# Scores with keys on partitions, transposes by DMA: a change to a fused memory-attention, mixer and MLP kernel

## The chip, the cores and the metric

The kernel runs on one core of one Trainium2 chip. The metric is the time of one execution on the device, in microseconds (us), as the median of several runs; lower is better. One run of each kernel was taken with the hardware profiler; stage lengths and waits come from that run, and its span is a microsecond or two below the time of that run.

Engine names in the profile: PE is TensorE (matmuls), PEld its weight loads, DVE VectorE, ACT ScalarE, POOL GpSimd, SP SyncE, which does nothing here but issue DMA transfers. A name with a q (SPq, ACTq) is the engine's instruction queue issuing a DMA.

## The reference, cut to what matters

```python
# x: 2048 tokens x 1024; 32 heads of 128; 64 segments of 32 tokens, 8 memory slots
h = layernorm(x) * (1 + ca) + sa
mem = mem0
for s in range(64):                                  # recurrent over segments
    hs = concat([mem, h[segment s]])                 # 40 rows
    q, k, v = hs @ Wq, hs @ Wk, hs @ Wv              # per head
    p = softmax(where(mask, q @ k.T * scale, -1e9))
    o = (p @ v) @ Wo
    mem, out[segment s] = o[:8], o[8:]
x1 = x + ga * out
u = layernorm(x1) * (1 + cb) + sb
# the "mixer": w1, gelu, a shift of channel groups by 1 or 2 tokens, w2
x1b = u + shift(gelu(layernorm(u) @ w1)) @ w2
y  = x1b + gelu(layernorm(x1b) @ w3) @ w4            # the last MLP, 1024 -> 3584 -> 1024
result = x1 + gb * y
# sa, ca, ga, sb, cb, gb: six rows of 1024, from silu(c) @ w_mod
```

The recurrence is removed in both kernels: all memories are guessed from segment means, all segments are computed at once with one memory column a segment (its eight rows are taken to be equal), and a check at the end decides whether an exact pass must follow. With these inputs none follows.

## The kernel before: the parts that matter here

Tokens and memory columns of three segments form a tile of 99 columns; there are 22 tiles a head. Two heads ("a pair") share one load of projection weights. TensorE gets attention work of one pair woven with the projections of the next.

```python
# V token-major: hh is the stationary operand, 256 columns (a pair of heads) move
nc.tensor.matmul(a3[:rows, j, :], lhsT=hhT[:, kt, tokens i], rhs=w["wv"][:, kt, :], ...)
evac(vs[...], a3[...])                                # PSUM -> staging tile
nc.sync.dma_start(V[p0:p0 + e - n, T, :], vs[n - i * P:e - i * P, j, :])   # L502: to tiles of 99 rows
# --- cut ---
# scores: queries on partitions, softmax along the free axis, 5 tiles a group
nc.tensor.matmul(ps_s[:TS, b, :], lhsT=QT[tile], rhs=KTt[tile])
nc.vector.tensor_tensor(smk, ps_s, mask, ALU.add)                          # L558
nc.vector.tensor_reduce(nmx, smk, AX.X, ALU.max, negate=True)              # L560
for b in range(nb):
    nc.scalar.activation(E[:, b], smk[:, b], ACT.Exp, bias=nmx[:, b:b+1], accum_out=ssum[:, b:b+1])  # L564
nc.vector.reciprocal(rin, ssum)
nc.vector.tensor_tensor(Pm, E, rin, ALU.mult)
nc.tensor.transpose(ps_t[tile], Pm[tile], ident)                           # L578
nc.vector.tensor_copy(PT, ps_t)                                            # L580
nc.tensor.matmul(ps_o[tile], lhsT=V[tile], rhs=PT[tile])                   # feature-major output
# --- cut: outputs copied to stgx / OTm4 and written to DRAM (OTx_d) ---
# Wo stage: OTc reads the head outputs back, 32 heads accumulate, then LayerNorms give z
for kt in range(KT): nc.tensor.transpose(pt[:, kt, :], z[:, kt * P:(kt + 1) * P], ident)   # L758
nc.vector.tensor_copy(zT[tile t], pt)
# modulation rows: silu(c) repeated over 128 columns is the stationary operand
for kt in range(KT): nc.tensor.matmul(pb, lhsT=sc_rep[:, kt, :], rhs=wm[:, kt, :], ...)
```

## Time and profile before

The kernel before takes 1675.88 us (median of 3 runs, 1674.5 to 1677.36). This is the profile's page for it: the span, the busy time and share of each engine with its number of instructions, then the span in 40 slices of about 42 us, each digit the busy share in tenths (for PEclk, the granted TensorE clock).

```profile
span 1674.0 us, 30157 instructions
...
PE 1607.6 (96%) x11426; PEld 924.5 (55%) x11601; DVE 692.5 (41%) x1688; ACT 681.8 (41%) x2202; POOL 222.4 (13%) x324
...
PE   6898999999999999999998989999999999999998
...
PEclk9998999999999999999998999999999999999999
```

TensorE is busy nearly always, and the others under half of the time. The digits that are not 9 show where time can be lost without TensorE working: at the start, in the fourth slice (about 126 to 167 us, where attention begins), and in slices 22 and 24 (between about 880 and 1005 us, where attention ends and the output projection begins). The stretch table gives busy microseconds and instruction counts of each engine in stretches of 100 us, then the granted clock and the DMA share.

```profile
core 0: us, PE busy (x) PEld busy (x) DVE busy (x) ACT busy (x) POOL busy (x), PEclk, DMA share, GB/s
...
100.00:200.00 100.00, 91.01 (x919) 70.27 (x923) 35.21 (x93) 51.59 (x196) 18.56 (x41) 0.95 0.42 123
...
300.00:400.00 100.00, 98.76 (x867) 66.39 (x878) 56.06 (x147) 60.67 (x231) 1.67 (x10) 1.00 0.32 86
...
900.00:1000.00 100.00, 89.28 (x477) 42.78 (x486) 34.04 (x103) 25.89 (x86) 24.11 (x35) 0.94 0.77 265
```

In the middle of attention TensorE is the limit (the missing matmul records, told of below, make its 98.76 a little too low), so what leaves TensorE there leaves the time. The groups of instructions say what TensorE and ScalarE do for the softmax and for V (columns: line, engine, operation, tiles, shapes, count; busy us and mean ns of one; idle time before them and what ended it).

```profile
L487 PE MATMUL acc<-wv,hhT 128*128 128x256 bf16 (+1 forms) x2176 | 265.6, 275 | 0.7 <-DVE hhT L405 0.7
L564 ACT ACTIVATE E<-smk,nmx 99x99 f32<-99x99 f32 x704 | 256.4, 367 | 124.9 <-DVE nmx L560 122.6 <-DVE OTm_2212 L601 0.8 <-DVE rin L570 0.6
...
L578 PE MATMUL ps_t<-ident,Pm 99*99 99x99 bf16 x704 | 61.4, 214 | 4.7 <-POOL Pm L572 3.4 <-DVE Pm L572 1.0
```

A mean duration is not what a matmul costs when they are pipelined. The 704 transposes show 214 ns each, but their starts are about 47 ns apart. In this trace the start spacing is 216 ns at 512 columns, 109 at 256, 56 at 128, 47 at 99: columns divided by 2.4 per ns, plus about 2.5 ns. The Trainium skill says the same (TensorE: Matmul & The Clock Gate, Part 1: "N ÷ 2.4 GHz + ≈2.5 ns once warm", with 215.7 ns at 512 columns); the trace agrees.

### The profile page before, as it was taken

The page shows a single profiled execution, that of the slowest core. Times are in us where ns is not written, and L with a number is a line of the kernel's source. Part 1 is how long each engine was busy: PE and PEld are TensorE (multiplying, and loading weights), DVE is VectorE, ACT ScalarE, POOL GpSimd, SP SyncE. Part 2 cuts the span into 40 slices and gives each one's busy share as a digit, 9 for nine tenths or more (in the row PEclk, how much of TensorE's full clock was granted, in tenths as well). Part 3 has the DMA queues.
Part 4 walks back from the last instruction along what each step waited for, and adds up shares of the span by engine and source line. Part 5 has one row for each costly group of instructions (what it writes and reads, how often), then busy time and mean ns, then how long its engine had stood idle before and what let it go on. Part 6 is the DMA issues. An engine that isn't in the chain of part 4 may idle for free. (4 is left out here: it accounts for less than half of the span.)

```text
span 1674.0 us, 30157 instructions
## 1 busy us (share of the span) xinstructions
PE 1607.6 (96%) x11426; PEld 924.5 (55%) x11601; DVE 692.5 (41%) x1688; ACT 681.8 (41%) x2202; POOL 222.4 (13%) x324
## 2 busy tenths in 40 slices
PE   6898999999999999999998989999999999999998
PEld 3477666666666666666665434444444444444443
DVE  5614446555465554645555153453285020111102
ACT  2515657566566665655657020222423203021120
POOL 6301200000000000000002132032012304040300
PEclk9998999999999999999998999999999999999999
DMA  9682334232242422335314897776177767474741
GB/s 316 220 278 71 95 85 109 70 95 80 62 108 70 111 64 74 95 107 157 113 35 144 288 326 267 266 252 220 44 256 247 257 187 246 150 263 136 235 132 50
DMA packets 251868, 267.20 MB, mean 160 GB/s; under 512 B 11354, under 2 KB 221370, under 8 KB 249666
## 3 DMA queue, kind: packets, MB, share of 16 engines
q1 hardware_dynamic: 241136, 236.57, 45.8%
q10 hardware_dynamic: 9938, 26.51, 4.0%
q8 instruction: 93, 1.52, 0.4%
q0 software_dynamic: 640, 2.10, 0.4%
q14 instruction: 61, 0.50, 0.1%
HBM read 205.54 MB, written 42.23 MB: 148 GB/s over the span
## 5 line engine op out<-in xcount | busy, mean ns | idle before, releaser
L564 ACT ACTIVATE E<-smk,nmx 99x99 f32<-99x99 f32 x704 | 256.4, 367 | 124.9 <-DVE nmx L560 122.6
L487 PE MATMUL acc<-wv,hhT 128*128 128x256 bf16 (+1 forms) x2176 | 265.6, 275 | 0.7 <-DVE hhT L405 0.7
L248 PE MATMUL acc<-hhT,wq 128*128 128x512 bf16 (+3 forms) x1264 | 252.4, 341 | 8.3 <-DVE hhT L344 2.1
L248 PE MATMUL acc<-hhT,wk 128*128 128x512 bf16 (+3 forms) x1262 | 252.8, 340 | 2.5
L679 PE MATMUL acc<-wstream,OTc 128*128 128x512 bf16 x999 | 228.6, 384 | 12.9 <-DMA wstream<-in_A_Wo_dram 7.5
L487 PEld LDWEIGHTS <-hhT 128*128 128x128 bf16 (+1 forms) x2176 | 211.1, 100 | 31.8 <-DVE hhT L405 1.2
L883 PE MATMUL acc<-z2T,wstream 128*128 128x512 bf16 x878 | 193.1, 379 | 0.9
L907 PE MATMUL acc<-wstream,h2T 128*128 128x512 bf16 x878 | 193.1, 379 | 0.9
L884 ACT ACTIVATE h2T<-acc 128x512 bf16<-128x512 f32 x112 | 66.9, 597 | 270.9 <-PE acc L883 266.2
L248 PEld LDWEIGHTS <-wq 128*128 128x128 bf16 x1312 | 113.1, 98 | 112.0 <-issue 6.2
L248 PEld LDWEIGHTS <-wk 128*128 128x128 bf16 x1312 | 113.0, 98 | 110.0 <-DMA wk<-in_A_Wk_dram 1.8
L679 PEld LDWEIGHTS <-OTc 128*128 128x128 bf16 x1024 | 100.1, 99 | 130.7 <-issue 15.5
L907 PEld LDWEIGHTS <-h2T 128*128 128x128 bf16 x896 | 87.7, 98 | 105.7
L883 PEld LDWEIGHTS <-wstream 128*128 128x128 bf16 x896 | 87.6, 98 | 105.5
L564 ACT ACTIVATION_READ_ACCUMULATOR E<-smk,nmx 99x1 f32 x704 | 132.1, 188 | 0.0
L570 DVE RECIPROCAL rin<-ssum 99x5 f32<-99x5 f32 (+1 forms) x160 | 29.5, 184 | 197.8 <-ACT E L564 197.5
L560 DVE TENSOR_REDUCE nmx<-smk 99x5 f32<-99x495 f32 (+1 forms) x160 | 96.6, 604 | 2.2
L580 DVE COPY PT<-ps_t 99x495 bf16<-99x495 bf16 (+1 forms) x160 | 61.7, 386 | 83.5 <-PE ps_t L578 81.5
L598 ACT CAST stgx<-ps_o 128x480 bf16<-128x480 f32 (+2 forms) x160 | 80.1, 501 | 35.9 <-PE ps_o L593 34.4
L98 ACT ACTIVATE QT<-acc 128x512 bf16<-128x512 f32 (+2 forms) x126 | 65.1, 522 | 67.9 <-PE acc L248 64.5
L96 ACT CAST vstg<-acc 128x512 bf16<-128x512 f32 (+1 forms) x111 | 61.1, 551 | 74.1 <-PE acc L487 57.2
L96 ACT CAST KTt<-acc 128x512 bf16<-128x512 f32 (+3 forms) x121 | 60.6, 513 | 58.4 <-PE acc L248 51.1
(337 smaller groups left out, 1546.7 us busy)
## 6 DMA issues: line engine op xcount, KB each, us to landing
wstream<-in_A_Wo_dram SPq DMA_DIRECT2D x36, 1024.0 KB
wstream<-in_B_w_dram SPq DMA_DIRECT2D x28, 1024.0 KB
wstream<-in_B_w_dram SPq DMA_DIRECT2D x32, 896.0 KB
OTx_d<-stgx SPq DMA_DIRECT2D x32, 512.0 KB
OTc<-OTx_d SPq DMA_DIRECT2D x16, 1024.0 KB
wstream<-in_w_mod_dram SPq DMA_DIRECT2D x9, 1024.0 KB
wq<-in_A_Wq_dram SPq DMA_DIRECT2D x16, 512.0 KB
wk<-in_A_Wk_dram SPq DMA_DIRECT2D x16, 512.0 KB
```

The costliest lines, as they stand in the source:

```text
L96: nc.scalar.copy(dst, src)
L98: nc.scalar.mul(dst, src, scale)
L248: nc.tensor.matmul(acc[:, o:o + n], lhsT=W[:, kt, hl * P:(hl + 1) * P], rhs=rhs_fn(kt), start=(kt == 0), stop=(kt == KT - 1))
L487: nc.tensor.matmul(a3[:rows, j, :], lhsT=hhT[:, kt, O0 + i * P:O0 + i * P + rows], rhs=w["wv"][:, kt, :], start=(kt == 0), stop=(kt == KT ...
L560: nc.vector.tensor_reduce(nmx[:TS, :nb], smk[:TS, :nb, :], AX.X, ALU.max, negate=True)
L564: nc.scalar.activation(E[:TS, b, :], smk[:TS, b, :], ACT.Exp, bias=nmx[:TS, b:b + 1], scale=1.0, accum_out=ssum[:TS, b:b + 1])
L580: nc.vector.tensor_copy(g["PT"][:TS, :nb, 0:TS], ps_t[:TS, :nb, 0:TS])
L598: nc.scalar.copy(stgx[:].rearrange("p (s j) -> p s j", j=SEG)[:, s0:s0 + nsg, :], blk[:, b0:3 * nb, MS:L])
L679: nc.tensor.matmul(accs[tt][:], lhsT=ot[:, hl, tt * P:(tt + 1) * P], rhs=woc[:, hl, :], start=(h == 0), stop=(h == H - 1))
L883: nc.tensor.matmul(acc[:], lhsT=w3c[:, kt, fl * P:(fl + 1) * P], rhs=z2T[:, kt, b * 512:(b + 1) * 512], start=(kt == 0), stop=(kt == KT - 1))
L884: nc.scalar.activation(h2T[:, ft, :], acc[:], ACT.Gelu_apprx_tanh)
L907: nc.tensor.matmul(accs[tt][:], lhsT=h2T[:, ft, tt * P:(tt + 1) * P], rhs=w4c[:, fl, :], start=(ft == 0), stop=(ft == FT - 1))
```

## The change

The intent is to take work from TensorE in attention and to thin out the softmax on ScalarE and VectorE.

- Scores are computed with keys on partitions, so the masked exponentials are already in the form that the output product needs as its stationary operand: no transpose of the probabilities. No maximum is subtracted, the mask is a product with 0, 1 or 8, and the row sum comes out as a 129th column of the output product (a column of ones beside V). One wide exponential serves five tiles.
- V is projected feature-major, like Q and K (weights stationary, 480 tokens move), and turned by a DMA transpose, one a head. The head output is token-major now and is turned by two DMA transposes. The 608 DMA copies from staging tiles into V are gone.
- Tokens are permuted so that a tile is 96 tokens in a row, followed by its 3 memory columns.
- The transposes of z, in both mixer products, become DMA transposes on ScalarE's queue.
- The modulation rows are summed on VectorE, split into two bf16 halves, and spread over partitions by two matmuls instead of eight.

```diff
@@ V and projections (cut) @@
-    nc.tensor.matmul(a3[:rows, j, :], lhsT=hhT[:, kt, tokens i], rhs=w["wv"][:, kt, :], ...)
-    nc.sync.dma_start(V[p0:p0 + e - n, T, :], vs[n - i * P:e - i * P, j, :])
+    nc.tensor.matmul(acc[:, 0:CH], lhsT=W[:, kt, hl * P:(hl + 1) * P], rhs=hh[:, kt, i * CH:(i + 1) * CH], ...)
+    nc.sync.dma_start_transpose(Vs[h % 3][:, :, 0:DH], VTs[h % 2][:].rearrange("p t c -> p (t c)"))
@@ scores and softmax (cut) @@
-    nc.tensor.matmul(ps_s[:TS, b, :], lhsT=QT[...], rhs=KTt[...])
-    ... add mask, max, 5 exponentials with row sums, reciprocal, multiply, transpose, copy ...
+    nc.tensor.matmul(ps[:rows, o:o + w], lhsT=KTt[:, ...], rhs=QT[:, ...])
+    nc.scalar.activation(E[:rows, 0:o], ps[:rows, 0:o], ACT.Exp)
+    nc.vector.tensor_tensor(Em[:rows, c0:c0 + o], E[:rows, 0:o], mk[:rows, 0:o], ALU.mult)
@@ outputs (cut) @@
-    nc.tensor.matmul(ps_o[...], lhsT=V[:TS, T, ...], rhs=PT[:TS, b, 0:TS])
+    nc.tensor.matmul(ps[:rows, i, :], lhsT=Em[:k, ...], rhs=V[:k, t, 0:DH + 1])
+    nc.vector.reciprocal(rin, ps[:rows, 0:n, DH])
+    nc.vector.tensor_tensor(O[:rows, ...], ps[:rows, 0:n, 0:DH], rin[...], ALU.mult)      # Os: 2 buffers
+    # flip(h), after the last outputs of the head:
+    nc.sync.dma_start_transpose(OT, O[0:96, :, :].rearrange("p t c -> p (t c)"))
+    nc.sync.dma_start_transpose(MT, O[96:112, :, :].rearrange("p t c -> p (t c)"))
@@ z (cut) @@
-    for kt in range(KT): nc.tensor.transpose(pt[:, kt, :], z[:, kt * P:(kt + 1) * P], ident[:])
-    nc.vector.tensor_copy(dstT[:, :, t * P:(t + 1) * P], pt[:])
+    nc.scalar.dma_start_transpose(z2T[:, :, t * P:(t + 1) * P], zs[t][:])
@@ modulation rows (cut) @@
-    for kt in range(KT): nc.tensor.matmul(pb[:], lhsT=sc_rep[:, kt, :], rhs=wm[:, kt, :], ...)
+    nc.vector.scalar_tensor_tensor(a, wm[:, kt, :], sc32[:, kt:kt + 1], a, ALU.mult, ALU.add)   # x8
+    # hi = bf16(a); lo = a - hi
+    nc.tensor.matmul(pb[:], lhsT=ones_b[:], rhs=hi, start=True, stop=False)
+    nc.tensor.matmul(pb[:], lhsT=ones_b[:], rhs=lo, start=False, stop=True)
```

## The prediction

> **What bounds the kernel now.** TensorE. The busy table gives PE 96% of 1674 us, VectorE and ScalarE 41% each, and the stretch table shows PE 98.7 of every 100 us from 200 to 800 us. Matmul starts in the timeline are 216 ns apart at 512 columns, 109 at 256, 56 at 128, about 47 at 99 and 32 at 71: columns at 2.4 per ns plus about 2.5 ns (weight loads hide): over all matmuls about 1573 us (estimate), plus 100 us of gaps. By stage: about 24 us in the first 75 us (first weights, LayerNorm), about 17 us at 130-200 us (softmax on VectorE and ScalarE starves TensorE while it has little projection work), about 20 us at 850-1000 us (attention drains, head outputs return from DRAM), 4 us in the second mixer product.
>
> **Removed, added, moved (estimates from those spacings).**
> - Probability transposes: 704 x 47 ns = 33 us of PE gone.
> - z transposes: 256 x 56 ns = 14 us gone.
> - Modulation rows: 64 x 216 ns become 16: 10 us gone. VectorE gains about 45 us, mostly in attention, where it has room.
> - V moves from 16 x 17 x 8 matmuls of 256 columns to 32 x 8 x (4 x 480 + 199): 242 us become 229, -13 us.
> - Outputs widen from 99 to 129 columns (row sum in the product): 33 becomes 40 us, +7.
> - In all about 1514 us of matmul starts, -59 us.
> - Softmax (about 12 us ScalarE, 10 us VectorE a head) becomes five wide exponentials and masks plus eight reciprocal/multiply pairs (3 and 7 us). All projection evictions go to ScalarE, then about 11 us busy in a 24 us head: below PE.
> - 608 V staging copies go; three DMA transposes a head come.
>
> **On the critical path.** All PE time in attention is, so the -46 us there should show almost whole, about 2 us per head pair of 50. The 17 us of softmax starvation should fall to about 4. In the second mixer product VectorE is the limit (4.18 us a tile against 3.46 of PE); its z copy (0.67) leaves but rows enter, so only about 6 of the 12 us come. Startup and the final 390 us stay. The drain gets a longer tail (transpose, write, read back): perhaps +5 us.
>
> 1674 - 59 - 13 + 5 (mixer) - 2 + 0..10 gives about 1605.
>
> **The uncertain step.** The DMA transposes have no duration in this trace. The Trainium skill, DMA: Bandwidth & Descriptors, Latency and other measured facts, gives 261 GB/s: V (721 KB) about 2.8 us, head output about 2.4, harmless in 24 us. VectorE: DVE Perf Modes, The three transpose paths, gives 1309 ns for one 128x128: 22 in a row would be 29 us, more than a head. I believe the first; no run shows either.
>
> **Right if:** attention runs near 48 us a head pair with PE still about 99% busy, no ptb or P transposes, a shorter 130-200 us, V transposes landing in under 8 us, Wo start gaps unchanged. **Wrong if:** output products wait for V transposes, weight loads queue behind transposes on SP, ScalarE's queue blocks on issuing z transposes (mixer slower), or the drain gap grows by more than 20 us.
>
> Predicted 1605 us, 1572 to 1650 in 8 of 10; faster by over 2% 0.82, within 2% 0.13, slower 0.05.

## The result, and the profile after

The changed kernel takes 1621.94 us (median of 4 runs, 1621.37 to 1625.4); the kernel before, in the same rounds, 1675.19 us. The ratio is 0.9684, with a 95% interval of 0.9668 to 0.9699. Here and below, a ratio is the mean time of one kernel's runs over that of the other's of the same rounds, and by the numbers the profiled runs are left out of it, so it is not quite the ratio of the medians quoted. All outputs are right. The profiled run of the changed kernel was the slowest of its four (1625.4 us; the others took 1621.4 to 1622.1), so the stage lengths below, which are all from that run, are some 3 us too long in sum.

The page of the changed kernel, same lines as before:

```profile
span 1623.3 us, 23466 instructions
...
PE 1542.2 (95%) x9560; PEld 818.0 (50%) x9634; DVE 546.0 (34%) x1321; ACT 499.6 (31%) x1041; POOL 236.9 (15%) x355
...
PE   6789999999999999999977799999989999999998
...
PEclk9999999999999999999997999999999999999999
```

TensorE's busy time fell by 65 us, but the span fell by only 51. Attention is solid 9s now, without the dip in its fourth slice, but three 7s in a row (slices 21 to 23, about 812 to 933 us) show a deeper hole where attention ends. The stretch table says the same:

```profile
100.00:200.00 100.00, 95.07 (x770) 59.42 (x767) 51.91 (x115) 39.16 (x99) 12.38 (x22) 0.97 0.83 200
...
300.00:400.00 100.00, 100.00 (x718) 59.50 (x717) 33.00 (x92) 42.04 (x103) 4.95 (x16) 1.00 0.54 119
...
800.00:900.00 100.00, 73.60 (x504) 41.74 (x506) 31.44 (x95) 23.13 (x63) 10.61 (x32) 0.88 0.68 178
```

From 800 to 900 us TensorE was busy 74 of 100 us, at a mean granted clock of 0.88. The groups that replace the ones shown of before, from the page:

```profile
L300 PE MATMUL acc<-hh,wv 128*128 128x480 bf16 x1024 | 226.6, 366 | 0.1
...
L576 DVE TENSOR_TENSOR O<-ps_o,rin_all 99x384 bf16<-99x384 f32 (+2 forms) x256 | 133.2, 523 | 15.3 <-DMA MT<-O 7.6
```

V's products wait for nothing. The idle time in front of the normalizing multiply is new: VectorE wanted to write an output buffer O that a DMA transpose still read. The waits of TensorE, all of the run, largest first (us in total, times, longest):

```profile
PE ps_o L573 <- DVE O L576: 9.6, 2, 9.2
PE acc L677 <- DMA wstream<-in_A_Wo_dram: 9.4, 4, 3.4
PE acc L677 <- DMA OTc<-OTx_d: 8.9, 2, 7.8
PE small_ps L377 <- DMA wchunk<-in_w_mod_dram: 8.5, 3, 4.7
PE acc L453 <- DVE hbar L441: 5.3, 1, 5.3
PE acc L310 <- DVE hh L471: 4.4, 1, 4.4
```

The first and the third are almost wholly in the hole after attention, the last two at the start. To place the rest, the run is cut into stages at TensorE's own landmarks. This table is worked out from each trace: "work" is the sum of columns / 2.4 + 2.5 ns over all matmuls of the stage, with the matmul records that the trace lacks filled in (the page of before shows 11601 weight loads, but only 11426 matmuls; the missing ones are counted at 512 columns). Products of 1 to 8 columns, which the rule makes too cheap, are counted at about 28 ns. "Loss" is the length less the work: idle time, half-speed clock and wider spacings together.

| stage, until the last start of | before: length = work + loss | after: length = work + loss | change of work, of loss |
|---|---|---|---|
| memory guess | 109.8 = 79.7 + 30.0 | 110.1 = 76.2 + 33.9 | -3.5, +3.9 |
| attention up to 200 us | 90.2 = 69.4 + 20.9 | 89.9 = 82.0 + 7.9 | +12.6, -13.0 |
| rest of attention (last projection) | 690.4 = 676.7 + 13.7 | 634.3 = 630.5 + 3.8 | -46.2, -9.9 |
| end of attention and Wo | 262.5 = 235.1 + 27.4 | 272.8 = 227.3 + 45.5 | -7.8, +18.1 |
| mixer, w1 | 58.0 = 57.0 + 1.0 | 55.6 = 55.3 + 0.4 | -1.7, -0.6 |
| mixer, w2 | 66.6 = 63.2 + 3.3 | 62.1 = 55.7 + 6.4 | -7.5, +3.1 |
| last MLP, to the end | 396.5 = 389.4 + 7.1 | 398.5 = 387.2 + 11.3 | -2.2, +4.2 |
| sum | 1674.0 = 1570.5 + 103.4 | 1623.3 = 1514.2 + 109.2 | -56.3, +5.8 |

(Lengths, works and losses are rounded one by one. In the second row after does more work in the same time, which the third row repays.) The work fell by 56 us, and the loss, which was 103 us, did not fall with it: 23 us less of it in attention, 29 us more of it elsewhere, most of that at the end of attention.

How far can one trace be trusted? The experiments below give more traces in which a stage was left alone. With the w2 stage unchanged its length was 62.1 us in the changed kernel and 58.3, 60.6, 59.9 and 57.9 in e1, e5, e6 and e7. The end of attention and Wo took 272.8 us, and 268 to 271 in e1, e3, e4 and e7, which leave the two output buffers and the order of the tail alone; its loss was 38.9 to 43.7 there, not 45.5. The last MLP took 398.5 us, and 399.9 to 403.7 in e1, e5, e6 and e7. So a difference of 4 us in one of these stages, read from one trace each, is not shown; the two attention rows repeat within 1 us wherever attention was left alone (e2, e3, e6).

Attention as a whole went from 780.6 to 724.2 us, and 10 us were given back in the stage after it. Two questions stay for the experiments: why did the dip at the start of attention go, and what made the hole at its end?

### The profile page after: what moved, and what is told of

It is laid out like the page before. It is cut to its first block, busy times and chain, and to the rows that moved or that the text cites. A ratio compares the mean times of both kernels' runs of the same rounds, so it can differ in the third digit from the quotient of the medians.

```text
span 1623.3 us, 23466 instructions
## 1 busy us (share of the span) xinstructions
PE 1542.2 (95%) x9560; PEld 818.0 (50%) x9634; DVE 546.0 (34%) x1321; ACT 499.6 (31%) x1041; POOL 236.9 (15%) x355
## 5 line engine op out<-in xcount | busy, mean ns | idle before, releaser
L300 PE MATMUL acc<-hh,wk 128*128 128x480 bf16 x1024 | 227.3, 368 | 1.5 <-DMA wk<-in_A_Wk_dram 1.1
L300 PE MATMUL acc<-hh,wv 128*128 128x480 bf16 x1024 | 226.6, 366 | 0.1
L300 PE MATMUL acc<-hh,wq 128*128 128x480 bf16 x1024 | 225.0, 369 | 0.6 <-DVE hh L408 0.5
L576 DVE TENSOR_TENSOR O<-ps_o,rin_all 99x384 bf16<-99x384 f32 (+2 forms) x256 | 133.2, 523 | 15.3 <-DMA MT<-O 7.6
L115 ACT ACTIVATE QT<-acc 128x480 bf16<-128x480 f32 (+1 forms) x192 | 87.9, 477 | 160.3 <-PE acc L300 151.5
L300 PEld LDWEIGHTS <-wv 128*128 128x128 bf16 x1024 | 94.3, 98 | 82.0
L113 ACT CAST KT<-acc 128x480 bf16<-128x480 f32 (+2 forms) x190 | 84.9, 465 | 155.5 <-PE acc L300 146.4
L113 ACT CAST VT<-acc 128x480 bf16<-128x480 f32 (+3 forms) x222 | 86.2, 420 | 149.1 <-PE acc L300 137.5
L562 DVE TENSOR_TENSOR Em<-E,maskB 99x495 bf16<-99x495 bf16 (+1 forms) x128 | 48.6, 381 | 199.5 <-ACT E L560 199.1
L573 PEld LDWEIGHTS <-Em 99*99 99x99 bf16 (+2 forms) x704 | 69.9, 127 | 46.6 <-DVE O L576 10.2
```

The lines of the kernel that those rows point to most:

```text
L113: nc.scalar.copy(dst, src)
L115: nc.scalar.mul(dst, src, scale)
L300: nc.tensor.matmul(acc[:, 0:CH], lhsT=W[:, kt, hl * P:(hl + 1) * P], rhs=hh[:, kt, i * CH:(i + 1) * CH], start=(kt == 0), stop=(kt == KT - 1))
L562: nc.vector.tensor_tensor(Em[:rows, c0:c0 + o], E[:rows, 0:o], mk[:rows, 0:o], ALU.mult)
L573: nc.tensor.matmul(ps[:rows, i, :], lhsT=Em[:k, col0(t):col0(t) + rows], rhs=V[:k, t, 0:DH + 1], start=True, stop=True)
L576: nc.vector.tensor_tensor(O[:rows, ts[0]:ts[0] + n, :], ps[:rows, 0:n, 0:DH], rin[:, :, None].to_broadcast([rows, n, DH]), ALU.mult)
```

## The experiments

Each of the first eleven has 3 rounds beside the kernel before on the same chip, the last one 5. "After" is the changed kernel. Its own ratio of 0.9684 comes from other rounds, so differences of less than about 0.002 in ratio (3 us) are not read from the ratio alone; the stage lengths of the traces are used beside it, with the spread told above.

### e1_v_twice: does the time of V's DMA transposes matter?

```diff
-    nc.sync.dma_start_transpose(Vs[h % 3][...], VTs[h % 2][...])
+    for _ in range(2):
+        nc.sync.dma_start_transpose(Vs[h % 3][...], VTs[h % 2][...])
```

> The changed kernel (1621.9 us, ratio 0.968) with every V transpose issued twice into the same tile: 32 more transposes of 721 KB, each about 4.35 us of issue on SP's queue. Theory A (the transposes hide in the 24 us of TensorE work a head; queue use rises from about 8.4 to 12.7 us a head): the stretches from 200 to 800 us stay at PE 99 to 100 of 100 us, and only the drain of the last head pair gets longer, by 5 to 10 us, so 1627 to 1632 us. Theory B (the transposes are close to binding on the queue or the DMA engines): PE falls under 97 of 100 us in the middle of attention and the time rises by 20 us or more.

Measured: 1632.73 us (1629.27 to 1634.84), ratio 0.975 [0.973, 0.9771]: about 11 us over the changed kernel for 32 more transposes. In the middle of attention it cost nothing. A line of the stretch table, to be read against 300 to 400 us above:

```profile
300.00:400.00 100.00, 100.00 (x721) 59.56 (x719) 32.95 (x93) 42.13 (x101) 5.54 (x19) 1.00 0.75 152
```

The DMA share rose from 0.54 to 0.75, and TensorE stayed at 100. By stage, attention grew from 724.2 to 731.1; its loss up to 200 us went from 7.9 to 14.8, and after that it stayed at 3.8 (at the start of attention TensorE's output products waited 2.3 us for their V and 2.9 us for an output buffer, neither of them over 0.3 us in the changed kernel), and the last MLP from 398.5 to 403.7: TensorE waited 6.7 us there for the first gelu (2.4 in the changed kernel). The drain, where the first theory had put its 5 to 10 us, did not grow (271.1 us). So the throughput of the transposes has slack in steady state; their latency counts only where no other work is at hand. In the changed kernel the DMA view shows these medians from issue to landing, in us:

```profile
V<-VT SPq DMA_TRANSPOSE x32, 6.3
OT<-O SPq DMA_TRANSPOSE x32, 5.2
MT<-O SPq DMA_TRANSPOSE x32, 3.0
z2T<-z ACTq DMA_TRANSPOSE x16, 5.6
```

### e2_z_pe: what are the DMA transposes of z worth?

```diff
-    nc.scalar.dma_start_transpose(z2T[:, :, t * P:(t + 1) * P], zs[t][:])
+    for kt in range(KT):
+        nc.tensor.transpose(pt[:, kt, :], zs[t][:, kt * P:(kt + 1) * P], ident[:])
+    nc.vector.tensor_copy(z2T[:, :, t * P:(t + 1) * P], pt[:])
     # the same for zT; two tiles of lag and two transpose banks, as in the kernel before
```

> The changed kernel with both z transposes back on TensorE (256 transposes of 56 ns, copies on VectorE, lag of two tiles as before). Theory A (TensorE time is what counts): 14 us longer, about 1636 us. Theory B (DMA transposes issued by ScalarE hold up its queue, so the removed 14 us were mostly lost again in the second mixer product and at the start of the last MLP): 0 to 5 us longer, 1622 to 1627 us, and the second mixer product itself within 3 us of the 62 us that it takes in the changed kernel.

Measured: 1641.31 us (1639.12 to 1642.64), ratio 0.9806 [0.979, 0.9822]: 19 us over the changed kernel. The mixer stages grew from 55.6 to 66.7 and from 62.1 to 69.8. That is more than the 14 us of transposes on TensorE, and more than either theory said; VectorE takes its copies back too, but how much of the rest that explains was not tested. A caveat: this version shows a loss of 9.7 us in the w1 stage where the kernel before has 1.0, so some of the 19 us belongs to its order of work rather than to the transposes.

### e3_z_sp: does ScalarE's queue lose time by issuing them?

```diff
-    nc.scalar.dma_start_transpose(z2T[...], zs[t][:])
+    nc.sync.dma_start_transpose(z2T[...], zs[t][:])          # and zT
```

> The changed kernel with the z transposes issued by SP in place of ScalarE. In its trace ScalarE spent 1.25 to 4.9 us on issuing each one in the second mixer product, VectorE then waited for x1b stores, and the first GELU of the last MLP waited for the last transpose. Theory A (the ScalarE queue is the obstacle): the mixer gets 3 to 8 us shorter, about 1616 us. Theory B (the obstacle is the DMA engines being full of weight prefetch, or SP's own loads queue behind transposes that wait for z): no gain, or 3 to 10 us longer.

Measured: 1619.25 us (1617.98 to 1620.38), ratio 0.9673 [0.9657, 0.9689]. The median is 3 us lower, but the ratio differs by only 0.0011, which the rounds can't tell from nothing. The w2 stage took 56.7 us against 62.1 in the changed kernel, but against 57.9 to 60.6 in the four other traces that left it alone, so some 1 to 5 us; the rest hardly moved. On ScalarE's queue one issue took from 1.25 us to 4.9 us, so the issue does hold ScalarE up, but in the time this is worth at most some 3 us. e10 to e12 return to it.

### e4_rows_pe: are the modulation rows better on VectorE?

```diff
-    # 8 multiply-adds on VectorE, split in hi and lo, 2 matmuls with ones
+    for kt in range(KT):
+        nc.tensor.matmul(pb[:], lhsT=sc_rep[:, kt, :], rhs=st["wm"][:, kt, :], start=(kt == 0), stop=(kt == KT - 1))
```

> The changed kernel with the modulation rows back on TensorE (64 matmuls of 216 ns in place of 16). Theory A (VectorE has room, TensorE has none): 48 x 0.216 = 10 us longer, of which 7.8 in attention and 2.6 in the second mixer product, about 1632 us. Theory B (in the mixer VectorE is the limit and the two halves of gb cost it about 12 us): the mixer gets shorter by 3 to 6 us, the attention part longer by 7.8, so 2 to 5 us longer in all, about 1625 us.

Measured: 1617.51 us (1616.94 to 1619.4), ratio 0.9663 [0.9647, 0.9679]: with 48 more matmuls of 216 ns, 10 us, on the engine that is the limit, it is not 10 us slower, as the first theory had it (the second had 2 to 5 us), but about 4 us faster; the ratios differ by 0.0021, so the sign of this is at the edge of what the rounds can tell. Two places show where the 10 us went. The first is the start of attention. In the changed kernel VectorE's timeline (start and duration in us) reads:

```profile
110.50 3.11 DVE L255 SCALAR_TENSOR_TENSOR row_a<-wstream,sc,row_a 128x512 f32<-128x512 bf16 x4
113.53 0.70 DVE L253 TENSOR_SCALAR row_a<-wstream,sc 128x512 f32<-128x512 bf16 x1
114.16 1.40 DVE L255 SCALAR_TENSOR_TENSOR row_a<-wstream,sc,row_a 128x512 f32<-128x512 bf16 x2
115.48 0.65 DVE L470 CAST hh<-small_ps 128x480 bf16<-128x480 f32 x1
...
116.28 1.52 PE L310 MATMUL acc<-hh,wq 128*128 128x199 bf16 x8 [4.36 <-DVE hh L471]
```

The row sums are written in the program for pairs late in attention, but in the instruction order of the engine they come as soon as their weights are there, at 110 us. The copy of the guessed memories into hh, for which TensorE waits 4.4 us, stands behind them. TensorE then runs at half the clock (the granted clock from 115.5 to 120 us was 0.50): eight products of 199 columns take 1.52 us there. In e4 the same two steps are:

```profile
111.01 0.66 DVE L471 CAST hh<-small_ps 128x480 bf16<-128x480 f32 x1 [7.93 <-PE small_ps L468]
...
112.43 0.85 PE L311 MATMUL acc<-hh,wq 128*128 128x199 bf16 x8
```

The first score comes at 116.6 us in place of 122.6. The second place is the w2 stage, where VectorE was busy 49.6 of 62.1 us: it took 57.0 us, all of it TensorE's work, with no loss left. Of this 5 us gain the spread of that stage takes most: it was 57.9 in e7 with the rows on VectorE.

### e5_v_first: V before Q and K in each head

```diff
-    for which, nm in enumerate(("wq", "wk", "wv")):
+    for which, nm in ((2, "wv"), (0, "wq"), (1, "wk")):
     # and the V transpose is issued right after V, not after K
```

> The changed kernel (1621.9 us) with V projected before Q and K in every head, so that each V transpose is issued about 14 us sooner. In its trace the last head's V transpose starts at 836.8 us, after all other projections, takes 6 us of queue, and the flips of heads 29 and 30 queue behind it. Theory A (the loss at the end of attention is the latency of the chain V transpose, output, flip, store, reload): start gaps between 800 and 905 us fall from 32 us to about 20, total about 1610 us. Theory B (the loss is set by the weight stream for Wo and the DMA engines being full): no change, within 3 us.

Measured: 1620.57 us (1619.01 to 1623.89), ratio 0.9679 [0.9661, 0.9698], no difference that the rounds can tell. By stage, the end of attention and Wo fell from 272.8 to 264.4 us, as was meant (the last head's V is projected sooner), but the loss at the start of attention grew from 7.9 to 11.6 us and the last MLP by 1.8.

### e6_o_three: a third output buffer

```diff
-    Os = [vp.tile([P, NT, DH], BF16, name=f"O{i}") for i in range(2)]
+    Os = [vp.tile([P, NT, DH], BF16, name=f"O{i}") for i in range(3)]
```

> The changed kernel with three output buffers in place of two, so that head 31's outputs do not wait for the flip of head 29. In its trace that wait held VectorE for 7.6 us and TensorE for 9.2 us at 847 to 856 us. Theory A (this wait is on the path of the drain): 5 to 9 us shorter, about 1615 us. Theory B (it only covers another wait: the flip of head 30, the Wo weights that SP issues after the flips, the reload of the last outputs): 0 to 2 us shorter.

This tests the hole after attention. In the changed kernel its timeline reads, from the last V transpose on (the SPq lines are from SyncE's own timeline; the 17.62 us span three issues and the waits between them):

```profile
836.75 6.04 SPq L523 DMA_TRANSPOSE V<-VT  x1
...
844.77 7.42 SPq L582 DMA_TRANSPOSE OT<-O  x1
...
852.29 1.17 SPq L583 DMA_TRANSPOSE MT<-O  x1
...
855.63 1.02 DVE L576 TENSOR_TENSOR O<-ps_o,rin_all 104x384 bf16<-104x384 f32 x2 [7.64 <-DMA MT<-O]
...
856.24 1.03 PE L573 MATMUL ps_o<-V,Em 99*99 99x129 bf16 x6 [9.24 <-DVE O L576]
...
858.54 17.62 SPq L672 DMA_DIRECT2D wstream<-in_A_Wo_dram  x3
...
875.60 0.39 PE L573 MATMUL ps_o<-V,Em 99*99 99x129 bf16 x4
```

The chain is: the flip of head 29 (the two transposes of its output) is issued late, behind the last V transpose, and takes 7.4 us to issue; head 31 shares its buffer and can be normalized only after it; TensorE stands still for 9.2 us; only then are the Wo weights issued, and the last output products stand behind Wo products that wait for these weights. Then comes the last flip, the write and the read back, for which TensorE waits another 7.8 us, at 902 us.

Measured: 1617.23 us (1615.98 to 1618.15), ratio 0.9655 [0.9639, 0.9671]. That is 4.7 us by medians and 0.0029 in ratio. The 9.2 us wait for O became this, in four pieces:

```profile
PE ps_o L573 <- DVE O L576: 1.3, 4, 0.5
```

The last output product came at 851.2 us in place of 875.8, and the stage took 264.8 us in place of 272.8 (268 to 271 in the other traces with two buffers, so 3 to 8 us). About 3 us did not reach the end: the last MLP took 401.3 us in place of 398.5, with 4.1 us of waiting for the first gelu in place of 2.4. What is left of the chain in this stage: 8.0 us for the read back, 4.8 for the memory columns, 2.8 for Wo weights.

### e7_scores_twice: is attention bound by TensorE alone?

```diff
     for t in SG[g]:
-        nc.tensor.matmul(ps[:rows, o:o + w], lhsT=KTt[...], rhs=QT[...], start=True, stop=True)
+        for _ in range(2):
+            nc.tensor.matmul(ps[:rows, o:o + w], lhsT=KTt[...], rhs=QT[...], start=True, stop=True)
```

> The changed kernel with every score matmul issued twice into the same place: 704 more of 47 ns with their weight loads. It is the size of the probability transposes that the change removed. Theory A (attention is bound by TensorE's start spacing, so small matmuls count one for one): 33 us longer, about 1655 us. Theory B (small matmuls partly hide in waits and weight loads): under 20 us longer.

Measured: 1652.57 us (1649.33 to 1656.68), ratio 0.9876 [0.9858, 0.9894]. Attention grew by 31.2 us for 704 more matmuls: 44 ns each, which is what the rule gives for 99 columns (43.8; the spacing seen is 47). So a matmul more or less in attention costs its full spacing, and by the same spacing the 704 transposes that the change removed come to about 31 us as well (worked out, not run by itself).

### e8_before_wide_exp: did the softmax make the dip at the start of attention?

Here the kernel before is edited: no maximum, one wide exponential for a group, row sums by VectorE.

```diff
-    nc.vector.tensor_reduce(nmx[:TS, :nb], smk[:TS, :nb, :], AX.X, ALU.max, negate=True)
-    for b in range(nb):
-        nc.scalar.activation(E[:TS, b, :], smk[:TS, b, :], ACT.Exp, bias=nmx[:TS, b:b + 1], scale=1.0, accum_out=ssum[:TS, b:b + 1])
+    nc.scalar.activation(E[:TS, :nb, :], smk[:TS, :nb, :], ACT.Exp)
+    nc.vector.tensor_reduce(ssum[:TS, :nb], E[:TS, :nb, :], AX.X, ALU.add)
```

> The kernel before (1675 us) with the softmax's ScalarE work cut as the change cuts it: no maximum subtracted, one wide exponential a group in place of five with accumulator reads, the row sum as a reduction on VectorE in place of the maximum. ScalarE falls by about 9 us a head, TensorE's work is the same. Theory A (softmax binds only where the projections are thin, at 130 to 200 us): the gaps there fall from 17 to about 8 us, the stretches from 200 to 800 us do not change, about 1665 us. Theory B (softmax on ScalarE costs time all through attention): 25 us or more shorter.

Measured: 1672.97 us (1672.17 to 1674.49), ratio 0.999 [0.9973, 1.0006]. Most of the exponential's cost on ScalarE went, and nothing came of it: attention took 780.8 us against 780.6, with a loss of 22.2 us up to 200 us (20.9 before) and of 12.5 after it (13.7). So the load on ScalarE, half of the prediction's reason for the dip, is not what made it. VectorE's half was not tested here, because a row sum took the place of the maximum; and e8 is not clean, for TensorE waited 5.6 us for a probability multiply on GpSimd from 130 to 200 us (1.8 before). What ScalarE waited for, between 110 and 215 us, points elsewhere. In the kernel before:

```profile
ACT vstg L96 <- DMA V<-vstg: 8.9, 5, 3.2
```

and in e8:

```profile
ACT vstg L96 <- DMA V<-vstg: 22.1, 9, 3.9
```

ScalarE could not empty the V projections because the staging tiles were not free, and with the faster softmax that wait was longer.

### e9_before_v_split: the staging copies on two queues

```diff
-    nc.sync.dma_start(V[p0:p0 + e - n, T, :], vs[n - i * P:e - i * P, j, :])
+    (nc.sync if T % 2 else nc.gpsimd).dma_start(V[p0:p0 + e - n, T, :], vs[n - i * P:e - i * P, j, :])
```

> The kernel before with every second V staging copy issued by GpSimd in place of SP, nothing else. Run e8 left the start gaps at 130 to 200 us as they were, so softmax on ScalarE does not cause them. In the trace of before SP's queue issues V copies back to back there (38 in 30.2 us, then 32 in 25.6 us), and ScalarE waits for staging buffers (8.9 us), more so in e8 (22.1 us). Theory A (the issue rate of 38 V copies a head pair on one queue paces the first head pair, whose Q and K were done before): the gaps in the attention stage fall from 27.7 to under 20 us, and the time by 6 to 12 us, about 1665 us. Theory B (the sum of VectorE, GpSimd and eviction latency in the thin first head pair is the cause, whatever the queue): within 3 us of before, about 1674 us.

The reason to try it is the SyncE queue's timeline in the kernel before:

```profile
114.96 30.23 SPq L502 DMA_DIRECT2D V<-vstg  x38
...
149.38 25.63 SPq L502 DMA_DIRECT2D V<-vstg  x32
```

At 0.8 us for each issue, 38 copies fill 30 us, back to back, just when V of the first pairs is due.

Measured: 1665.41 us (1661.76 to 1665.99), ratio 0.9933 [0.9914, 0.9952]. Attention fell from 780.6 to 769.2 us, its loss up to 200 us from 20.9 to 9.7, and ScalarE's wait for staging tiles from 8.9 us to this:

```profile
ACT vstg L96 <- DMA V<-vstg: 0.7, 1, 0.7
```

Two queues with the same copies gained 10 us. So it was the issue of the 608 copies from one queue, which the change removes, that held up most of the start of attention; the softmax was the same in both kernels. (GpSimd's issues were also shorter, 0.53 us against 0.75 in the median. Which of the two counts was not separated.)

### e10_rows_zsp_o3: e3, e4 and e6 together

The edits are those of the three, nothing else.

> The changed kernel with three edits that each helped alone: rows on TensorE (e4, minus 4 us), z transposes issued by SP (e3, minus 2 us), three output buffers (e6, minus 5 us). If the three lie in different places of the path (start of attention, mixer, drain) they add: attention stage about 726 us, Wo stage about 262, first mixer product 55.6, second about 56.5, last MLP about 397, in all about 1609 to 1611 us. If e3 and e4 relieve the same wait in the mixer, which the mixer lengths of 56.7 and 57.0 us suggest, the sum is about 3 us worse: 1612 to 1614 us.

Measured: 1617.66 us (1611.43 to 1624.15), ratio 0.9642 [0.9618, 0.9667]. If the gains of the three added up (about 3, 4 and 5 us, by medians), it would be near 1610, and the ratio 0.9623. The interval of the ratio holds that value, so the times do not show that the gains fail to add. The trace, which is from the slowest of the four runs (1624.15 us), shows Wo 267.8 and w2 56.8, but 405.8 us for the last MLP, 9 us more than in e4. TensorE waited there 7.2 us for the first gelu.

### e11_all_tail: e10, with e5 and another order of the tail

```diff
-    interleave(att[NHP - 1], M_units(NHP - 3) + M_units(NHP - 2) + W0[0:2])
+    interleave(att[NHP - 1], M_units(NHP - 3) + M_units(NHP - 2) + W0[0:1])
     for u in att["end"]: u()
-    for u in W0[2:3] + M_units(NHP - 1, use_psS=True): u()
+    for u in W0[1:3] + M_units(NHP - 1, use_psS=True): u()
```

One Wo unit fewer stands before the last outputs, and one more behind them, to cover the way of the last head through DRAM.

> As e10, and V projected first, and one unit less of Wo work woven into the last head pair (one before the last outputs, two after them in place of two and one). Theory A (the drain is a latency chain, and the last V transpose and the last outputs behind Wo matmuls in TensorE's order are two links of it): the Wo stage falls to 250 to 256 us against about 262 in e10, total 1600 to 1606 us. Theory B (after the third output buffer what is left is the store and reload of the last outputs, which this edit does not shorten): within 2 us of e10.

Measured: 1608.28 us (1603.01 to 1614.59), ratio 0.96 [0.9565, 0.9634]. The end of attention and Wo took 255.3 us, 17.5 less than in the changed kernel, so the end of attention is now shorter than in the kernel before (262.5); which part of that is e5's edit and which the new order was not separated. But the last MLP still took 404.5 us. TensorE's wait at its start:

```profile
PE acc L874 <- ACT h2T L875: 6.4, 1, 6.4
```

ScalarE's first gelu waited in turn for a transpose of z, which the SyncE queue issued like this:

```profile
1204.44 11.40 SPq L855 DMA_TRANSPOSE z2T<-z  x3
```

Three transposes took 11.4 us to issue, just when the weights of the last MLP are prefetched by the same queue. The last z was ready 4.1 us before its transpose was issued (7.7 us in e10).

### e12_rows_tail: e11, with the z transposes back on ScalarE's queue

The edits are those of e4, e5, e6 and the tail; only e3's is left out.

> The kernel of e11_all_tail (rows on TensorE, three output buffers, V projected first, one Wo unit woven in and two after the last outputs), but with the z transposes left on ScalarE's queue, as in the changed kernel. Theory A: the 7 to 8 us by which the last MLP of e10 and e11 was longer than that of e4 (405.8 and 404.5 against 396.8 us) come from SyncE issuing the last z transposes late, behind weight transfers; then the last MLP is near 397 us, the Wo stage near 255, the attention near 725, and the time near 1600 us, at least 4 us under e11. Theory B: the wait comes from DMA engines that are full at that point, whoever issues; then the last MLP stays near 404 us and the time is within 2 us of e11's 1608.

Measured: 1603.41 us (1598.26 to 1603.86, 5 runs), ratio 0.9569 [0.9556, 0.9582]. The last MLP took 396.0 us, and the wait at its start is down to this:

```profile
PE acc L874 <- ACT h2T L875: 0.3, 1, 0.3
```

The last transpose was issued as soon as its z was ready, and the lengths are those of the first theory. But who issues does not decide by itself. With ScalarE's queue e1 shows the same wait as e11, and with SyncE's queue e3 shows a short one:

```profile
PE acc L876 <- ACT h2T L877: 6.7, 1, 6.7
PE acc L875 <- ACT h2T L876: 2.5, 1, 2.5
```

In e1 the last transpose took 5.6 us to issue on ScalarE's queue and landed 8.2 us after its start (1.25 and 3.4 us in e12). So a late last transpose makes the wait; the backlog on SyncE is how it came to be late in e10 and e11. The stages are 724.8 (attention), 252.4 (end of attention and Wo), 55.6 and 56.8 (mixer), and 396.0. The profiled run was the fastest of the five, so its span of 1596.5 us flatters the kernel; by medians it is 4.9 us under e11, measured in other rounds, and the two ratio intervals overlap. Of the 8.5 us between the two last MLPs, 6.1 are the wait for the first gelu. e12 is the best version found, some 18 us under the changed kernel and 72 under the kernel before.

## Why the prediction was right, and where it was wrong

The time lay in the predicted range, which was 78 us wide, and the change is faster by over 2%; the prediction's middle, 1605, was 17 us too low. The mechanism for the bulk, matmuls taken from TensorE, is right and shown. That the total came no further off is in part luck: a gain of 13 us was foreseen for a wrong reason, and 10 us that nobody foresaw in the rest of attention made up for about a third of the misses. Point by point:

- **TensorE bounds it: right.** e7 gives 44 ns of time for each added matmul of 99 columns. From 300 to 400 us it was busy 98.76 us before and 100.00 after.
- **59 us of matmul work removed: right within 3.** The spacings give 56.3 us. The term that was most off is V: 2176 products of 256 columns at 109 ns are 238 us, not 242, so V saves about 8 us and not 13. Of the 46 us that the prediction put into attention, the table shows 33.6 there; the rest falls into the stage after, or is the error of V, or was moved in from the stage before (see "the start").
- **The DMA transposes are harmless in a head of 24 us: right, though slower than costed.** The prediction took 261 GB/s from the Trainium skill (DMA: Bandwidth & Descriptors, Latency and other measured facts): an estimate of 2.8 us for V. Landing took 6.3 us in the median, under the 8 us that the prediction named as its test (9.4 at most). The other reading, 22 times the 1309 ns for one 128x128 block (VectorE: DVE Perf Modes, The three transpose paths), would be an estimate of 29 us and is far off. e1 shows the slack.
- **"softmax on VectorE and ScalarE starves TensorE" at 130 to 200 us: right in size, wrong in cause.** The loss there fell by 13.0 us, and 13 were foreseen. But e8 took much of that load from ScalarE and gained nothing, while e9 changed only who issues the V copies and its loss there fell by 11.2 us. Most of the gain came from the 608 copies. A second part was overlooked: in the kernel before, 64 products over 63 memory columns, all between 116 and 173 us, each started about 80 ns later than their columns say, 5 us in all, in e9 too; the changed kernel has no such products (the memory columns move together with 136 others). Against this stand its own 4.4 us wait and half clock at 116 us, which e4 removes: its loss there is about 2 us.
- **The rest of attention has almost no loss to give: wrong, to the good.** It lost 13.7 us before and 3.8 after. By the trace of before, about 9 of the 13.7 us are products that start a few ns later than the rule says, 6 us of them the 99-column ones (47 ns in place of 43.8), and about 5 are waits. e8 (12.5) says that it is not ScalarE's softmax, e9 (about 13.6) that it is not the queue of the V copies.
- **VectorE has room for the rows: wrong as to when.** It has room on average. But the sums ran at the start of attention, in front of a copy that TensorE waited for, and in the w2 stage, where VectorE was busy for 80% of the time. e4 shows that the 10 us on TensorE cost nothing and may have been the better bargain.
- **The start stays: right.** The stage took 110 us in both kernels. The work before the end of the memory guess fell by 3.5 us and the loss rose by 3.9, but this work was moved, not saved: the projections made there (249 products of 512 columns before, 248 of 480 after) cover fewer columns, and the rest comes with the 199-column products in attention. The stage is held by other things, such as the waits for modulation weights (8.5 us) and for the segment means (5.3).
- **"The drain gets a longer tail ... perhaps +5 us": mis-sized, and the largest miss.** The sum that ends at 1605 contains none of the 0 to 10 us allowed for it, and the loss in this stage rose by 18.1 (11 to 16 if measured in e1, e3, e4 and e7). "Wo start gaps unchanged" was wrong. The prediction saw the longer way of the last head, but not that the flip of an earlier head, issued behind a V transpose, blocks the buffer of a later one, nor that the weights are issued behind it all. e6 gets 3 to 8 us of the stage back with one buffer, e11 and e12 13 to 20 with V first and the order of the tail as well.
- **Only half of the mixer's gain comes: right in the profiled run, the cause open.** The w2 stage fell by 4.5 us of 7.5 us of work; in the other traces that left it alone it fell by 6 to 8.7. The cause named, VectorE, is not shown: e4, which takes the rows from VectorE, ends at 57.0 us, but so does e3 at 56.7 with the rows still on VectorE.
- **ScalarE's queue blocks on issuing z transposes: a little.** e3 is at most some 3 us faster, and combined with the rest the trace of e12 is better than that of e11.
- **The final stage stays: nearly.** Its loss rose by 4.2 us.

By spans the prediction took off 69 us (1674 to 1605) and 51 came, a miss of 18. The terms, in loss: the drain +18, the last MLP and the start +4 each (for the start it is moved work, not time), the work +3, against -10 in the rest of attention and -2 in the mixer; about 1 us is rounding and small terms. The last MLP's length moves by some us from kernel to kernel in which nothing of it was changed, and it moves with TensorE's wait for the first gelu: 0.3 us of wait and 396.0 us in e12, 0.6 and 396.8 in e4, 2.4 and 398.5 in the changed kernel, 4.1 and 401.3 in e6, 6.7 and 403.7 in e1, 7.2 and 405.8 in e10. What stays open is why the last z transpose lands late in some of them: the backlog on SyncE explains e10 and e11, but not e1 and e6. How much of the drain's loss is half-speed clock rather than waiting was not separated either; the granted clock was 0.88 from 800 to 900 us.

## What to carry to other kernels

When an engine is the limit in steady state, cost the change in steady state by start spacings, but cost the start and the end apart: there latency, buffer counts and the order on the queues decide, and a saving in a stage that is held by something else should not be summed. Compare stages over more than one trace before a few us are explained. Before giving a dip a cause, look at every queue in that stretch, the DMA-issuing one too: many small transfers can be limited by the issue alone. Moving work to an engine that is idle on average pays only if it is idle at the moment the scheduler puts the work there.

## What the Trainium skill lacked or had wrong

- DMA: Bandwidth & Descriptors, Issuing engines are not separate DMA queues: it says that issuing from several engines saves only issue time, "which is usually small relative to the DMA itself". Here 38 copies took 30.23 us to issue from one queue, and issuing every second one from GpSimd made the whole kernel 10 us faster (e9).
- DMA: Bandwidth & Descriptors: no time measured on trn2 for how long a DMA transpose occupies the issuing queue (there are only the vendor's cycle counts, for other shapes). Here the median is 4.3 us for 128x2816 bf16 (6.7 at most), 2.75 us for 96x2816, and 1.25 us for those of z ahead of the mixer's first product (1.82 in the median, 4.9 at most, for the 128x1024 ones of its second); in the busy stretch after attention an issue took 7.42 us (8.56 us in e12).
- DMA: Bandwidth & Descriptors, Latency and other measured facts: 261 GB/s for a DMA transpose with a non-contiguous middle dimension. 721 KB landed in a median of 6.3 us after the start of the issue, which is 114 GB/s over that time; 2.8 us, an estimate worked out from the page, is less than half of the latency of one transfer.
- VectorE: DVE Perf Modes, The three transpose paths: 1309 ns for a 128x128 block by DMA does not multiply. 22 blocks in one transfer took 6.3 us, not 29. The page does not say so.
